# The second Fourier stage's middle channel: a one-row matmul product replaced by a per-token bias in ScalarE's copy

## The chip, the cores and the metric

The kernel runs on one core of one Trainium2 chip. The metric is device time in microseconds, from a program's start to its end, as the median of several runs. A profile is one further execution, with a record of every instruction of every engine. The engines are PE (TensorE, with its weight loads shown as PEld), DVE (VectorE), ACT (ScalarE), POOL (GpSimd) and SP (SyncE, which here only issues DMAs). A DMA can be issued from the queue of several engines; in this kernel nearly all are issued by SyncE, and a few by ScalarE.

## The reference

Eight batches of 576 tokens, eight heads of 64 channels each, all in fp32. An attention of the linear kind comes first, then a Fourier mix with a layer norm and an MLP:

```
q_s = softmax(q, over the head's 64 channels);  k_s = softmax(k, over the 576 tokens)
attn = q_s @ (k_s^T @ v)                       # per batch and head
x  = attn as (8, 576, 512)                     # tokens x channels
u  = x + real(fft(fft(x, over tokens), over channels))
un = (u - mean(u)) / sqrt(var(u) + 1e-6)       # over the 512 channels
out = u + max(un @ w_ch1, 0) @ w_ch2           # 512 -> 2048 -> 512
```

The real part of the two-dimensional transform splits into a cosine product minus a sine product. The first stage, over tokens, makes Z, a cosine part and a sine part of each channel (or sum of channels). The second stage multiplies Z with cosines and sines over channels.

## The kernel before, in words

**Work around the change.** The kernel walks through the eight batches, in two phases. In the first it reads and converts weights, computes the attention of batches 0 and 1 and the MLP of batch 0, and prepares weights for the later batches. In the second a steady rhythm runs: while the MLP of one batch fills TensorE (products of L1544 for the up and down halves, L1641, L1671, with results named `ba`, `bb` and `bc`), the attention, the two Fourier stages and the layer norm of the next batch are worked in between. The MLP products use Strassen-like sums of quarter blocks, so VectorE and GpSimd make operands (L1514, L1555, L1617, L1621, L1678).

**The order is written out by hand.** Each piece of work is a list of steps with planned times (the `steps` and `at(...)` lists in the program's last function, and `timed` for batches 2 to 7). The steps are sorted by planned time and issued under a manual schedule, and every engine then works its own queue strictly in that order. Whatever waits at the head of a queue holds everything behind it. Semaphores order engines against each other. A DMA signals its end on one of eight completion semaphores, which are handed round over all DMAs of the SyncE and ScalarE queues in the order of the script.

**First Fourier stage.** `block` (batch 1, one channel block k at a time) and `blocks` (batches 2 to 7) multiply folded tokens by cosines and sines (`ft`). k = 0 and 1 are the cosine halves of the channels, k = 2 and 3 the sine halves, and k = 4 (`KT`) is the single middle channel, which has a cosine part only and so is one row. In `blocks` the products go to two two-bank PSUM buffers taken from `two()`: one holds the cosines (k = 0, 1, 4), the other the sines (k = 2, 3). The last products are `tails`, L1234, 20 in a batch. ScalarE then copies PSUM to SBUF in `copies(k, part)`:

- part "own" (L1246) makes `Z[b]` for k = 0 to 3, 256 of a batch's own tokens wide, and `Zr` for k = 4, one row of 256;
- part "shared" (L1249, L1250) makes `ZT` for k = 0 to 3 and `ZTr` for k = 4. These are the mirrored tokens that two batches share; batch b writes the half `W*(b%2)` of 64 columns each, so that an odd batch completes the pair.

The order of both parts over k is 2, 3, 0, 1, 4.

**Second Fourier stage.** `second` builds one mix: `mix_own(b, c)` for c = 0, 1 (128 tokens each), and `mix_shared(p)` once for each pair of batches. A mix is, on TensorE, four products of Z with `cd` (the channel cosines and sines; L1264) into one bank, 128 tokens by 512, and a fifth product, L1267, which adds the middle channel. Its left operand is a 128-row tile whose rows but the first stay zero (`Zr`, `ZTr`), and its right one has 129 columns, so that to each token the row's value is added in the cosine half, with a sign that alternates over the frequencies. After the products, `copy` (L1273) has ScalarE move the sine half to SBUF in the tile `sn`. `sums` (L1281) then has VectorE make cosine minus sine and cosine plus sine, and L1282 the two end columns. `adds` adds the result to x. In an odd batch the shared mix comes third, and in batch 7 it comes first.

**Around it.** After the mixes stand the norm (`norm`: statistics L1343 on VectorE, normalisation L1359 on ScalarE for the first batches, transposes L1365 on PE in batch 1) and the MLP of that batch. SyncE's queue around batch 1 holds the loads of the next batch's values (`vt`, L689, eight 32-token pieces in `values_to`), and stores of prepared weight sums (`w1s`, L452 and L455 and `w2s`, L455, in `combine`), with later loads of the same (L476). VectorE works on the weight sums at L449.

Of the kernel before, what the change touches and what calls it, by code (L numbers as in the profile page):

```python
# [46 lines left out]
P = 128  # L47
# [91 lines left out]
class _Block:  # L139
    def __init__(self, ctx, tc, q, kT, v, w1, w2, ft, cd, out):  # L140
        self.nc, self.tc = tc.nc, tc
        self.q, self.kT, self.v, self.w1, self.w2, self.out = q, kT, v, w1, w2, out
        self.ft_dram, self.cd_dram = ft, cd
        nc = self.nc
        pool = lambda name, **kw: ctx.enter_context(tc.tile_pool(name=name, bufs=1, **kw))
        self.const, self.work, self.small = pool("const"), pool("work"), pool("small")
        self.open_banks = []
        self.banks(0)
        ctx.callback(lambda: [p.__exit__(None, None, None) for p in self.open_banks[::-1]])
        self.dram = pool("dram", space=bass.MemoryType.DRAM)  # L150
        c = self.const
        self.ident = c.tile([P, P], F32, name="ident")
        make_identity(nc, self.ident[:])
        self.eps = c.tile([P, 1], F32, name="eps")
        nc.gpsimd.memset(self.eps[:], LN_EPS)
        self.pairs = []
        for b in range(2):
            t = c.tile([P, NR, DH + 1], F32, name=f"pairs{b}")
            (nc.vector if b else nc.gpsimd).memset(t[:], 1.0)
            self.pairs.append(t)  # L160
        self.sn = []
        for i in range(2):
            t = c.tile([P, NN], F32, name=f"sn{i}")
            nc.gpsimd.memset(t[:], 0.0)
            self.sn.append(t)

        self.ZT = c.tile([P, KT, P], F32, name="ZT")

        self.Zr, self.ZTr = c.tile([P, HD], F32, name="Zr"), c.tile([P, P], F32, name="ZTr")
        for t in (self.Zr, self.ZTr):  # L170
            nc.gpsimd.memset(t[:], 0.0)
        self.kb = c.tile([P, NR, 4, NC * Q], F32, name="kb")
        kb = self.kb[:].rearrange("p r g s -> p (r g s)")
        self.kss = [kb[:, i * NC * P:(i + 1) * NC * P].rearrange("p (c n) -> p c n", n=P) for i in range(NR)]
        self.vt = c.tile([P, NC, 2 * P + 3], F32, name="vt")

        self.T, self.F = c.tile([P, 2 * NR, 4, NT], F32, name="T"), c.tile([P, 2 * NR, P + W], F32, name="F")
        nc.gpsimd.memset(self.T[:], 0.0)
        nc.gpsimd.memset(self.F[:], 0.0)

        self.sign = c.tile([P, 1], F32, name="sign")
        nc.gpsimd.memset(self.sign[:], -1.0)
        nc.gpsimd.memset(self.sign[0:W], 1.0)
        d = self.dram
        self.w1s = [d.tile([P, 7, HD], F32, tag=f"w1s{p}", name=f"w1s{p}", bufs=1) for p in range(NP)]
        self.w2s = d.tile([7, P, NP, HD], F32, tag="w2s", name="w2s", bufs=1)

        self.w2d = d.tile([P, len(DEEP), GT], F32, tag="w2d", name="w2d", bufs=1)
        self.plan, self.base = [], {}
        for at in range(1, B + 1):  # L190
            self.base[at] = len(self.plan)
            self.plan += [self.w1s[p][:].rearrange("p a n -> p (a n)") for pair in PAIRS for p in pair]
            one = lambda m: self.w2s[WB_AT[m]].rearrange("p a n -> p (a n)")
            first = self.first_deep(at)
            self.plan += [one(m) for m in (ORDER if at == 1 else (1, 2) if at == B else (1,))]
            if at > 1:
                for i in range(first, len(DEEP), 4):
                    self.plan.append(self.w2d[:, i:min(i + 4, len(DEEP)), :].rearrange("p a n -> p (a n)"))
            if at == B:
                self.plan.append(one(4))  # L200

        self.big = c.tile([P, 3 * NF * D], F32, name="big")
        self.fifth = self.big[:, 3 * NF * D - 5 * P:3 * NF * D - P].rearrange("p (r n) -> p r n", n=P)
        nc.gpsimd.memset(self.fifth[0:64], 0.0)
        part = lambda i: self.big[:, i * NF * D:(i + 1) * NF * D].rearrange("p (f n) -> p f n", n=D)
        self.w1sb, self.w2sb, self.h0 = part(0), part(1), part(2)
        self.ft = c.tile([P, 4 * NM], F32, name="ft")
        self.cd = c.tile([P, 5 * QD + 1], F32, name="cd")
        self.xs, self.live, self.stream = {}, {}, {}
        self.turns = 0  # L210
        self.eo, self.unT, self.Z = {}, {}, {}
        self.unused = None
        self.pairs_used = []

        self.later = []

        self.words = [self.work.tile([P, 2, D], F32, tag=n, name="words", bufs=k) for n, k in (("xs", 2), ("x", 4), ("x", 4))]
# [928 lines left out]
    def block(self, b, k):  # L1146
# [26 lines left out]
        def copies():  # L1173
            pz, Z = box.pop(), self.Z[b]
            z, zt = (self.Zr[0:1], self.ZTr[0:1]) if k == KT else (Z[0:n, k, :], self.ZT[0:n, k, :])
            nc.scalar.copy(paired(z), interleaved(pz[:, NT - 1:NT - 1 + 2 * ME])[:, 0:P, :])

            at = W * (b % 2)
            nc.scalar.mul(paired(zt[:, at:at + Q]), interleaved(pz[:, 0:2 * MO])[:, 0:NT - 1, ::-1],
                          -1.0 if sines else 1.0)  # L1180
            nc.scalar.copy(paired(zt[:, at + Q:at + W]), interleaved(pz[:, 0:2 * ME])[:, NT - 2::-1, ::-1])

        return [(0, times), (1.4, copies)]

    def blocks(self, b):

# [50 lines left out]
        def copies(k, part, copy=nc.scalar.copy):  # L1237
            n, sines, Z = {3: QD - 1, 4: 1}.get(k, P), k in (2, 3), self.Z[b]
            z, zt = (self.Zr[0:1], self.ZTr[0:1]) if k == KT else (Z[0:n, k, :], self.ZT[0:n, k, :])
            flat = box[sines][0:n].rearrange("p a n -> p (a n)")  # L1240
            odd, even = place(k, 1).start, D + place(k, 0).start

            def both(x, y, size, step=1):
                return bass.AP(flat.tensor, flat.offset + x, [flat.ap[0], [step, size], [y - x, 2]])
            if part == "own":
                copy(paired(z), both(odd + NT - 1, even + NT, P))  # L1246
                return
            w = W * (b % 2)
            nc.scalar.mul(paired(zt[:, w:w + Q]), both(even, odd, NT - 1), -1.0 if sines else 1.0)  # L1249
            nc.scalar.copy(paired(zt[:, w + Q:w + W]), both(even + NT - 1, odd + NT - 2, NT - 1, -1))  # L1250

        return own, tails, copies, early, sine

    def second(self, z, zr, adds, two=True, apart=None):

        nc, V = self.nc, self.nc.vector
        cd, box = self.cd, []

        def times():
            banks = apart() if apart else [self.acc((P, D), two)] * 2  # L1260
            parts = (1, 0, QD), (0, QD, QD + 1), (2, NN + QD - 1, QD), (3, NN, QD - 1)
            for k, at, size in (parts[2], (3, HD, QD), *parts[:2]) if apart else parts:
                rows, pm = QD - 1 if k == 3 else P, banks[k > 1]
                nc.tensor.matmul(pm[:, at:at + size], lhsT=z(k)[0:rows], rhs=cd[0:rows, at:at + size], start=True,  # L1264
                                 stop=(k != 0))
                if k == 0:
                    nc.tensor.matmul(pm[:, at:at + size], lhsT=zr(), rhs=cd[:, D:], start=False, stop=True)  # L1267
            box.extend(banks)

        def copy():  # L1270
            sn = self.sn[self.turns % 2]
            self.turns += 1
            nc.scalar.copy(paired(sn[:, 0:HD]), interleaved(box.pop()[:, HD:]))  # L1273
            box.append(sn)

        def sums():
            pm, sn = box
            two = self.halves()
            a = interleaved(pm[:, 0:2 * (QD + 1)])[:, 0:QD, :]
            for i, op in enumerate((ALU.subtract, ALU.add)):  # L1280
                V.tensor_tensor(out=paired(two[:, i * NN + 1:(i + 1) * NN]), in0=a, in1=paired(sn[:, 1:NN]), op=op)  # L1281
# [14 lines left out]

    def mix_shared(self, p):
        return self.second(lambda k: self.ZT[:, k, :], lambda: self.ZTr[:],
                           [lambda lo, hi: self.added(self.xshared(p), hi, lo)])

    def mix_own(self, b, c):
        s = slice(c * P, (c + 1) * P)
# [4 lines left out]
            t = self.two()  # L1307
            return [t[:, 0, :], t[:, 1, :]]

        return self.second(lambda k: self.Z[b][:, k, s], lambda: self.Zr[:, s], adds, apart=None if b else apart)  # L1310

    def norm(self, g):

# [520 lines left out]
def kernel(ctx: ExitStack, tc: tile.TileContext, q, kT, v, w1, w2, ft,  # L1834
# [3 lines left out]
    def timed(t, order, g):  # L1838
# [12 lines left out]
        for k, dt in ((2, 0), (3, 0.9), (0, 4.4), (1, 4.6), (4, 6.4)):  # L1851
            steps.append((t + soon + dt, lambda k=k: own(k)))
        steps.append((t + soon + 6.6, tails))
        for i, k in enumerate((2, 3, 0, 1, 4)):
            for j, part in enumerate(("own", "shared")):
                steps.append((t + soon + 7.8 + 0.2 * i + 1.0 * j, lambda k=k, part=part: copies(k, part)))
        mixes = [blk.mix_own(b, c) for c in range(2)]
# [73 lines left out]
    t = 0  # L1931
# [62 lines left out]
```

## Time and profile before

| | |
|---|---|
| median of three timed runs | 1006.84 us (1006.43 to 1006.99) |
| profiled execution, span from first to last instruction | 1006.6 us |
| PE busy in the profiled execution | 995.6 us, 99% |
| PEld busy | 855.7 us, 85% |
| DVE busy | 718.6 us, 71% |
| ACT busy | 493.2 us, 49% |
| POOL busy | 442.9 us, 44% |
| granted TensorE clock | 1.000 |

The profiled execution has no other time of its own than the span. In the rows that are quoted below, L12 is line 12 of the kernel, `xN` the number of instructions in a group, and `a<-b` the tile written and the tiles read. A row of the timeline begins with the start in us from the start of the span and the duration in us; where instructions of one kind that follow each other are put together (`x4`), the duration is from the first's start to the last's end. In square brackets stand the idle time of that engine just before, and what ended it.

### The profile page before, as it was taken

The page shows a single profiled execution, that of the slowest core. Times are in us where ns is not written, and L with a number is a line of the kernel's source. Part 1 is how long each engine was busy: PE and PEld are TensorE (multiplying, and loading weights), DVE is VectorE, ACT ScalarE, POOL GpSimd, SP SyncE. Part 2 cuts the span into 40 slices and gives each one's busy share as a digit, 9 for nine tenths or more (in the row PEclk, how much of TensorE's full clock was granted, in tenths as well). Part 3 has the DMA queues.
Part 4 walks back from the last instruction along what each step waited for, and adds up shares of the span by engine and source line. Part 5 has one row for each costly group of instructions (what it writes and reads, how often), then busy time and mean ns, then how long its engine had stood idle before and what let it go on. Part 6 is the DMA issues. An engine that isn't in the chain of part 4 may idle for free.

```text
span 1006.6 us, 19808 instructions
## 1 busy us (share of the span) xinstructions
PE 995.6 (99%) x7562; PEld 855.7 (85%) x7562; DVE 718.6 (71%) x1356; ACT 493.2 (49%) x1277; POOL 442.9 (44%) x445
## 2 busy tenths in 40 slices
PE   8999999999999999999999999999999999999998
PEld 6844464888888899889988998899889998998897
DVE  6898898666765887588756877688667945685563
ACT  4585642872468228832775177625772342151200
POOL 4263420357535637664655465655646450040000
PEclk9999999999999999999999999999999999999999
DMA  9987499687989666975677577847753765674573
GB/s 300 258 281 245 158 240 346 205 243 226 342 283 272 230 230 219 266 237 210 251 220 242 206 269 237 253 174 270 231 204 135 267 213 200 224 265 172 183 256 132
DMA packets 123559, 236.37 MB, mean 235 GB/s; under 512 B 24184, under 2 KB 88440, under 8 KB 112840
## 3 DMA queue, kind: packets, MB, share of 16 engines
q1 hardware_dynamic: 123096, 234.58, 71.0%
q8 instruction: 60, 0.98, 0.4%
q14 instruction: 35, 0.29, 0.1%
q10 hardware_dynamic: 288, 0.26, 0.1%
q0 software_dynamic: 80, 0.26, 0.1%
HBM read 199.94 MB, written 39.06 MB: 237 GB/s over the span
## 4 chain that ended last, share of the span: by engine, by line
PE 87%; DVE 7%; ACT 3%; DMA 1%; issue 1%; SPq 0%; POOL 0%; DVEq 0%; POOLq 0%
PE bb L1544 16%; PE ba L1544 11%; PE bc L1544 11%; PE bb L1671 10%; PE ba L1671 7%; PE bc L1671 7%; PE bb L1641 5%; PE bc L1479 2%; PE bb L1760 2%; PE two L840 2%; PE one L755 2%; PE two L1207 1%; PE two L1264 1%; PE ba L1479 1%; PE bc L1760 1%; PE ba L1760 1%
## 5 line engine op out<-in xcount | busy, mean ns | idle before, releaser
L1544 PE MATMUL bb<-unT,big 128*128 128x256 f32 x768 | 183.3, 380 | 0.0
L1544 PEld LDWEIGHTS bb<-unT,big 128*128 128x128 f32 x768 | 144.8, 190 | 20.7 <-DVE u L1514 0.7
L1556 ACT ACTIVATE big<-big 128x512 f32<-128x512 f32 x96 | 59.8, 629 | 147.6 <-DVE big L1555 141.0
L1544 PE MATMUL ba<-unT,big 128*128 128x256 f32 x512 | 123.9, 382 | 0.0
L1544 PE MATMUL bc<-unT,big 128*128 128x256 f32 x512 | 121.5, 380 | 0.1
L817 ACT ACTIVATE qT<-q 32x128 f32<-32x128 f32 x384 | 117.9, 307 | 5.9 <-DVE q L807 0.8
L1544 PEld LDWEIGHTS bc<-unT,big 128*128 128x128 f32 x512 | 96.9, 190 | 13.7 <-DVE big L1555 0.5
L1544 PEld LDWEIGHTS ba<-unT,big 128*128 128x128 f32 x512 | 95.5, 190 | 13.9 <-issue 0.5
L1514 DVE TENSOR_TENSOR u<-bb,s 128x512 f32<-128x512 f32 x66 | 45.2, 685 | 85.0 <-PE bb L1544 66.5
L1671 PE MATMUL bb<-big 128*128 128x128 f32 x848 | 103.8, 276 | 0.2 <-DVE u L1678 0.2
L1671 PEld LDWEIGHTS bb<-big 128*128 128x128 f32 x848 | 98.9, 192 | 1.0 <-DVE u L1678 1.0
L1390 POOL COPY unT<-unT 32x256 f32<-32x256 f32 x98 | 42.0, 428 | 90.2 <-DVE unT L1382 85.9
L1621 POOL TENSOR_TENSOR x<-x,big 128x512 f32<-128x512 f32 x45 | 60.9, 1368 | 46.0 <-DVE big L1678 19.7
L1617 DVE TENSOR_TENSOR big<-big 128x512 f32<-128x512 f32 x98 | 79.9, 842 | 0.0
L1671 PE MATMUL ba<-big 128*128 128x128 f32 x640 | 79.0, 276 | 0.0
L1671 PEld LDWEIGHTS ba<-big 128*128 128x128 f32 x640 | 75.0, 192 | 0.8
L1390 ACT COPY unT<-unT 32x256 f32<-32x256 f32 x126 | 50.7, 402 | 31.3 <-DVE unT L1382 29.5
L804 POOL TENSOR_TENSOR q<-q,qm 128x512 f32<-128x512 f32 x24 | 25.8, 1073 | 88.2 <-DVE qm L799 53.1
L405 POOL TENSOR_TENSOR big<-big 128x512 f32<-128x512 f32 x24 | 30.4, 1268 | 68.4 <-ACT big L1556 68.4
L1641 PE MATMUL bb<-big 128*128 128x256 f32 x256 | 58.3, 379 | 0.0
L1555 DVE TENSOR_TENSOR big<-bc,u 128x512 f32<-128x512 f32 x64 | 44.0, 688 | 17.3 <-PE bc L1544 16.4
L1641 PEld LDWEIGHTS bb<-big 128*128 128x128 f32 x256 | 48.0, 190 | 6.1
(336 smaller groups left out, 1917.9 us busy)
## 6 DMA issues: line engine op xcount, KB each, us to landing
big<-w2d SPq DMA_DIRECT2D x67, 1024.0 KB, 4.6
big<-w1s SPq DMA_DIRECT2D x64, 896.0 KB, 4.7
big<-w2s SPq DMA_DIRECT2D x16, 1024.0 KB, 4.8
big<-in_w_dram SPq DMA_DIRECT2D x21, 512.0 KB, 6.0
w2d<-big SPq DMA_DIRECT2D x42, 256.0 KB, 6.5
kb<-in_kT_dram SPq DMA_DIRECT2D x28, 320.0 KB, 7.8
q<-in_q_dram SPq DMA_DIRECT2D x28, 256.0 KB, 6.0
vt<-in_v_dram SPq DMA_DIRECT2D x84, 80.0 KB, 2.7
```

Source lines behind the costliest of these rows:

```text
L405: e1.tensor_tensor(out=to(4), in0=at(2), in1=at(3), op=ALU.add)
L817: nc.scalar.activation(to[t, i * Q:i * Q + Q], one, ACT.Exp)
L1390: copy(to, of)
L1514: plus = lambda t: V.tensor_tensor(out=temp(t), in0=box["bb"][:], in1=box["s1"][:], op=ALU.add)
L1544: nc.tensor.matmul(bank()[:, i, :], lhsT=w[:, WA_AT[m], k * P:(k + 1) * P], rhs=self.unT[g][:, B_AT[m], k, :], start=first and i == 0 and ...
L1555: steps = [(0, lambda: V.tensor_tensor(out=hp(i), in0=bank()[:], in1=u()[:], op=ALU.add)), (0.8, lambda: nc.scalar.activation(hp(i), hp(i) ...
L1556: (0.8, lambda: nc.scalar.activation(hp(i), hp(i), ACT.Relu))]
L1617: e.tensor_tensor(out=to(o), in0=to(x), in1=to(y), op=op)
L1621: E.tensor_tensor(out=x, in0=x, in1=tile(m), op=ALU.add)
L1641: nc.tensor.matmul(box[name][:, i, :], lhsT=h[p][:, A_AT[m], i * P:(i + 1) * P], rhs=self.stream[n][:, p, :], start=p == 0 and (m != 1 or ...
L1671: nc.tensor.matmul(box[place[n]][:, i, :], lhsT=own(m)(A_AT[n])[:, f, :], rhs=w[:, r // 2, r % 2 * P:r % 2 * P + P], start=first and f == ...
L1760: nc.tensor.matmul(bank()[:, i, :], lhsT=h[p][:, A_AT[m], i * P:(i + 1) * P], rhs=w[:, p, :], start=first and i == 0 and p == 0, stop=p == ...
```

## The change

Batches 1 to 7 drop the fifth product; batch 0's two own mixes keep it (`column=None`). In its place:

- `column(name, row)` turns a row of PSUM results that has been copied to SBUF (`Zr`, `ZTr`) into a column over partitions. It issues one DMA for each 128 tokens, from ScalarE's queue: two for `Zr` (tile `zc`), one for `ZTr` (tile `zt`, in odd batches, when the pair is complete). That is 18 DMAs in all. It returns a step for GpSimd that writes the negated column beside it. The tiles have one buffer each.
- In `blocks` the columns are issued behind the row copies, and the order of the copies over k becomes 4, 2, 3, 0, 1, so that the rows are copied first. GpSimd's negation (`blk.minus`) gets its place 11.5 after the first products. In `block` (batch 1) the columns follow the copies of k = 4, and the negation comes at 3.
- In `second` ScalarE no longer copies the sine half but the cosine half: one plain copy of the even columns, and two `Identity` activations of the odd ones, with the column or its negation as the bias for each partition (token). VectorE's sums then read the sine half directly from PSUM, and the cosine half from `sn`. The end columns come from `sn` too.

```diff
@@ block (batch 1)
+            if k == KT:
+                box.extend([self.column("zc", self.Zr[0:1]), self.column("zt", self.ZTr[0:1])])
+
+        return [(0, times), (1.4, copies)] + [(3, lambda: [f() for f in box])] * (k == KT)
-        return [(0, times), (1.4, copies)]
@@ blocks (batches 2 to 7), copies
                 copy(paired(z), both(odd + NT - 1, even + NT, P))
+                if k == KT and b:
+                    self.minus = [self.column("zc", z)]
                 return
...
+            if k == KT and b % 2:
+                self.minus.append(self.column("zt", zt))
@@
+    def column(self, name, row):
+        nc, n = self.nc, row.shape[1] // P
+        t = self.small.tile([P, 2, n], F32, tag=name, name=name, bufs=1)
+        for i in range(n):
+            nc.scalar.dma_start(t[:, 0, i:i + 1], row[:, i * P:(i + 1) * P])
+        self.columns[name] = t
+        return lambda: nc.gpsimd.tensor_scalar(out=t[:, 1], in0=t[:, 0], scalar1=-1.0, scalar2=None, op0=ALU.mult)
@@ second, times
-                                 stop=(k != 0))
-                if k == 0:
+                                 stop=(k != 0 or not whole))
+                if k == 0 and whole:
                     nc.tensor.matmul(pm[:, at:at + size], lhsT=zr(), rhs=cd[:, D:], start=False, stop=True)
@@ second, copy
-            nc.scalar.copy(paired(sn[:, 0:HD]), interleaved(box.pop()[:, HD:]))
+            if whole:
+                nc.scalar.copy(paired(sn[:, 0:HD]), interleaved(box.pop()[:, HD:]))
+                box.append(sn)
+                return
+            pm, (t, i) = box.pop(), column()
+            nc.scalar.copy(sn[:, 1:NN:2], pm[:, 0:QD])
+            for j in range(2):
+                nc.scalar.activation(sn[:, 2 * j:NN:4], pm[:, QD + j:HD + 1:2], ACT.Identity, bias=t[:, j, i:i + 1])
             box.append(sn)
@@ second, sums
+            if not whole:
+                s = pm[:, HD + QD:]
+                s = bass.AP(s.tensor, s.offset, [s.ap[0], [1, QD], [1 - QD, 2]])
+                for i, op in enumerate((ALU.subtract, ALU.add)):
+                    V.tensor_tensor(out=paired(two[:, i * NN + 1:(i + 1) * NN]), in0=paired(sn[:, 1:NN]), in1=s, op=op)
+                ends = two[:, 0:2 * NN].rearrange("p (i n) -> p i n", i=2)[:, :, ::HD]
+                V.tensor_copy(ends, sn[:, ::HD].unsqueeze(1).to_broadcast([P, 2, 2]))
+                box.append(two)
+                return
@@ timed (batches 2 to 7)
-        for i, k in enumerate((2, 3, 0, 1, 4)):
+        steps.append((t + soon + 11.5, lambda: [f() for f in blk.minus]))
+        for i, k in enumerate((4, 2, 3, 0, 1)):
             for j, part in enumerate(("own", "shared")):
                 steps.append((t + soon + 7.8 + 0.2 * i + 1.0 * j, lambda k=k, part=part: copies(k, part)))
```

More of the change, by code (lines that the diff above doesn't have):

```diff
@@ L209, in __init__ @@
         self.xs, self.live, self.stream = {}, {}, {}
-        self.turns = 0
+        self.turns, self.columns = 0, {}
         self.eo, self.unT, self.Z = {}, {}, {}
@@ L1250, in copies, with second @@
             nc.scalar.copy(paired(zt[:, w + Q:w + W]), both(even + NT - 1, odd + NT - 2, NT - 1, -1))
+            if k == KT and b % 2:
+                self.minus.append(self.column("zt", zt))
         return own, tails, copies, early, sine
-    def second(self, z, zr, adds, two=True, apart=None):
+    def column(self, name, row):
[5 more added lines that the diff above has]
+        return lambda: nc.gpsimd.tensor_scalar(out=t[:, 1], in0=t[:, 0], scalar1=-1.0, scalar2=None, op0=ALU.mult)
+    def second(self, z, zr, adds, two=True, apart=None, column=None):
         nc, V = self.nc, self.nc.vector
         cd, box = self.cd, []
+        whole = column is None
         def times():
@@ L1298, in mix_shared @@
         return self.second(lambda k: self.ZT[:, k, :], lambda: self.ZTr[:],
-                           [lambda lo, hi: self.added(self.xshared(p), hi, lo)])
+                           [lambda lo, hi: self.added(self.xshared(p), hi, lo)], column=lambda: (self.columns["zt"], 0))
     def mix_own(self, b, c):
@@ L1308, in apart @@
             return [t[:, 0, :], t[:, 1, :]]
-        return self.second(lambda k: self.Z[b][:, k, s], lambda: self.Zr[:, s], adds, apart=None if b else apart)
+        return self.second(lambda k: self.Z[b][:, k, s], lambda: self.Zr[:, s], adds, apart=None if b else apart,
+                           column=(lambda: (self.columns["zc"], c)) if b else None)
     def norm(self, g):
```

## The prediction

> **What bounds the kernel now.** I read the page's busy times and its chain first, then a table of busy time by stage, then the timeline around each use of the product that goes.
>
> ```profile
> span 1006.6 us, 19808 instructions
> PE 995.6 (99%) x7562; PEld 855.7 (85%) x7562; DVE 718.6 (71%) x1356; ACT 493.2 (49%) x1277; POOL 442.9 (44%) x445
> PE 87%; DVE 7%; ACT 3%; DMA 1%; issue 1%; SPq 0%; POOL 0%; DVEq 0%; POOLq 0%
> ```
>
> TensorE is busy 99% of the span, and 87% of the chain that ends last is PE. The table by stage (stretch, length, then each engine's busy time) says whether there are gaps in which lost time could be made good.
>
> ```profile
> 150.00:180.00 30.00, 29.89 (x95) 16.10 (x94) 24.34 (x57) 11.64 (x27) 1.71 (x1) 1.00 0.91 314
> 460.00:565.00 105.00, 105.00 (x911) 96.66 (x910) 76.03 (x141) 58.66 (x162) 60.98 (x59) 1.00 0.72 235
> 565.00:780.00 215.00, 215.00 (x1861) 197.99 (x1861) 156.75 (x299) 120.18 (x333) 123.36 (x120) 1.00 0.65 220
> ```
>
> PE has no gap at all from 460 to 780 us. So a product taken off PE is worth its whole time, and a microsecond for which PE is held costs a whole microsecond, because PE takes its work in order. The question is therefore what the 18 products cost, and whether the new copies and transfers hold PE. I add the terms to the profiled span of 1006.6; the three timed runs have their median 0.24 us above it, at 1006.84, and I carry that 0.24 along.
>
> **What is removed.** This is batch 4, from its last first-stage products to the first second-stage mix. Columns: start, duration, engine, line, operation.
>
> ```profile
> 455.85 1.00 PE L1234 MATMUL two<-ft,eo 17*128 17x145 f32 x20
> 456.70 1.20 ACT L1246 COPY Z<-two 128x256 f32<-128x256 f32 x4 [0.57 <-PE two L1234]
> 456.79 1.86 PEld L1671 LDWEIGHTS ba<-big 128*128 128x128 f32 x16
> 457.75 0.36 ACT L1246 COPY Zr<-two 1x256 f32<-1x256 f32 x1
> 457.77 2.94 POOL L1617 TENSOR_TENSOR unT<-big,unT 128x512 f32<-128x512 f32 x2
> 458.02 0.18 ACT L1249 ACTIVATE ZT<-two 128x32 f32<-128x32 f32 x1
> ...
> 458.26 0.16 ACT L1250 COPY ZT<-two 127x32 f32<-127x32 f32 x1
> ...
> 458.57 0.53 PEld L1264 LDWEIGHTS two<-cd,Z 128*128 128x128 f32 x4
> ...
> 459.01 0.30 PEld L1267 LDWEIGHTS two<-cd,Zr 128*128 128x128 f32 x2
> ...
> 459.68 1.87 PEld L1671 LDWEIGHTS bb<-big,unT 128*128 128x128 f32 x16
> ...
> 462.79 0.75 DVE L1281 TENSOR_TENSOR eo<-two,sn 128x256 f32<-128x256 f32 x2
> ```
>
> A mix is five products, two records each. Ten records fill 458.57 to 459.68, 0.111 us each, so one product is 0.222 us. Batches 1 to 7 have 14 own mixes and 4 shared ones: 18 x 0.222 = 4.0 us off PE.
>
> **What holds PE in batches 3 to 7.** A mix writes into the two-bank buffer that held the sine products. It may start when ScalarE has read the last of them, the second ZT copy pair (the 127-row one): 458.26 + 0.16 = 458.42 before, 0.15 us ahead of PE at 458.57. That margin is all there is. The change puts the one-row copy Zr first, behind it two column DMAs issued by ScalarE itself, then the four Z, then ZTr (in odd batches with a third DMA), and only then the ZT pairs. What does an issue cost ScalarE? The trace has two, near the end:
>
> ```profile
> L1821 ACTq EVENT_SEMAPHORE x2: 17/17/17, 963.9 to 992.2; - x2
> L1821 ACTq DMA_DIRECT2D out_dram<-x x2: 360/366/373, 967.7 to 998.3; - x2
> DMA to landing us min/median/max: 1.7/1.7/1.7
> ```
>
> Those move 128 rows; a column has 128 elements, also one piece for each partition, so I take 0.37 us. The bound below is a bare queue event, 0.02. With t counted from 456.70, the start of the Z copies: Zr must await the last four of the 20 records of L1234, about (1.00 - 0.28) / 19 = 0.04 apart (0.28 is the overlap of the last, an estimate), so 0.15. It ends at 0.15 + 0.36 = 0.51; the DMA awaits that, 0.05 for the signal (an estimate); two issues bring 1.30. Four Z at 0.26 (from 456.70 to 457.75) bring 2.35, ZTr 0.15 more, the two ZT pairs 0.40 (from 458.02 to 458.42), a signal 0.05: PE may start at 2.95. Before it started at 458.57, which is 1.87. PE is held for 1.08 us in batches 4 and 6. In 3 and 5 the third issue adds its wait for the ZTr copy (0.10), a signal and 0.37: 1.60. Against 0.44 and 0.67 saved there, the nets are +0.64 and +0.93 each.
>
> Batch 7 mixes the shared tokens first, which need the last ZT pair, and that now stands behind a copy (L1685) of the main work:
>
> ```profile
> 772.98 1.20 ACT L1246 COPY Z<-two 128x256 f32<-128x256 f32 x4 [0.57 <-PE two L1234]
> ...
> 775.06 0.52 PEld L1264 LDWEIGHTS two<-cd,ZT 128*128 128x128 f32 x4
> ...
> 775.16 0.37 ACT L1685 COPY s<-ba 128x256 f32<-128x256 f32 x1 [0.15 <-PE ba L1671]
> ...
> 776.39 1.87 PEld L1671 LDWEIGHTS bb<-big,unT 128*128 128x128 f32 x16
> ```
>
> ZT can start at 3.02; three pairs 0.45, the L1685 copy 0.27, the last pair 0.25, a signal 0.05: 4.04 against 2.08 before, +1.96. This mix shrinks from 1.33 to 8 x 0.111 = 0.89, the two others save 0.44: net +1.08. Batches 3 to 7 together: 2 x 0.93 + 2 x 0.64 + 1.08 = +4.22.
>
> **Batch 2** has room:
>
> ```profile
> 242.66 1.20 ACT L1246 COPY Z<-two 128x256 f32<-128x256 f32 x4 [3.30 <-PE two L1234]
> ...
> 246.09 0.63 PEld L1264 LDWEIGHTS two<-cd,Z 128*128 128x128 f32 x4
> ```
>
> 242.66 + 2.95 = 245.61, 0.48 before PE gets there. It saves 0.44.
>
> **Batch 1: the transfers' semaphores.** Eight completion semaphores are handed round over all of SyncE's and ScalarE's DMAs in the order of the script, and an issue waits for the DMA that had its semaphore before. In the listing of the built program the script places the three columns among the eight vt loads of batch 2's values:
>
> ```
> SP   L689  DMA vt<-in_v      (7th of 8)   waits DMAHW4 = 208, which the first zc column raises
> SP   L689  DMA vt<-in_v      (8th)        waits DMAHW5 = 208, the second zc column
> SP   L453  DMA w1s<-big                   waits DMAHW7 = 208, the zt column
> ```
>
> SyncE ran well ahead of that place:
>
> ```profile
> 133.22 0.31 SPq L689 DMA_DIRECT2D vt<-in_v_dram  x1
> 134.94 0.31 SPq L689 DMA_DIRECT2D vt<-in_v_dram  x1
> 135.30 0.42 SPq L452 DMA_DIRECT2D w1s<-big  x1
> ...
> 138.90 0.40 SPq L455 DMA_DIRECT2D w1s<-big  x1
> DMA to landing us min/median/max: 4.5/4.5/4.5
> ...
> 139.00 0.16 ACT L1181 COPY ZTr<-acc 1x32 f32<-1x32 f32 x1
> ...
> 143.37 0.32 SPq L476 DMA_DIRECT2D big<-w1s  x1
> 144.74 0.50 SPq L455 DMA_DIRECT2D w2s<-spare  x1
> ...
> 152.00 0.76 DVE L449 TENSOR_TENSOR spare<-big 128x256 f32<-128x256 f32 x2 [1.87 <-DMA w2s<-spare]
> ...
> 159.40 2.23 ACT L1359 ACTIVATE eo<-x,mv,std 128x512 f32<-128x512 f32 x3 [0.44 <-DVE mv L1343]
> ...
> 160.26 0.14 PEld L1365 LDWEIGHTS tr<-ident,eo 128*128 128x128 f32 x1 [0.25 <-ACT eo L1359]
> ```
>
> (The 4.5 is the landing of the store at 138.90.) The seventh vt load went at 133.22. Now it waits for a column issued when ScalarE is past 139.16 and landed 1.7 us later: 140.9. Behind it in SyncE's queue stand the eighth load, six w1s stores, a w1s load that awaits their landing, and the w2s stores. From the seventh load, 0.3 for each vt and 0.5 for each store, the last store goes at about 143.9 instead of 138.90, and lands at 148.4; everything from 143.37 on is 5.0 us late. VectorE already waited 1.87 us for the w2s store; it now waits to about 157. Behind that wait in VectorE stand the statistics of batch 1, then ScalarE's normalisation (159.40), whose first 0.81 us releases PE's transpose at 160.26 with nothing to spare. PE stands still, and the 0.67 saved in this batch goes into the same wait: net +5.0. Below, if the last store lands in 1.7 like the ScalarE store, the term is +2.2. Above, if a column takes as long as the slowest small load,
>
> ```profile
> q<-in_q_dram SPq DMA_DIRECT2D x12, 64.0 KB, 7.1
> ```
>
> it is 5.0 + 5.4 = +10.4. I take 5.0, since the DMA engines are nearly idle while SyncE is held.
>
> [...]
>
> **What else is added** costs nothing while it is covered. Three ScalarE instructions for one in a copy, under 0.6 us more: in batch 4 the sums at 462.79 wait for PE's next product. GpSimd's negation stands behind its work until 457.77 + 2.94 = 460.71, and the columns have landed by then (456.70 + 0.56 + 0.74 + 1.7 = 459.70); the second bias copy awaits it, and nothing urgent stands behind either. If a column took 7.1 us, that cover would be gone, and VectorE's sums would be about 1 us late in each batch. The sums and the end copy on VectorE keep their sizes.
>
> **Sum.** -0.44 (batch 2) + 4.22 (3 to 7) + 5.0 (batch 1) = +8.8: 1006.6 + 0.24 + 8.8 = 1015.6 us.
>
> **Rivals.**
> *Issues cost ScalarE almost nothing* (0.02). The held time shrinks to 0.38, 0.55 and, in batch 7, a net of 0.03; batches 3 to 7 become -0.33, the sum +4.2: 1011.1. Against it stand the 360 to 373 ns rows, which are of a queue that had nothing behind them. [...]
> *Batch 1 takes no harm*: VectorE's wait at 152.00 does not lengthen. Then -0.67 - 0.44 + 4.22 = +3.1: 1009.9. It would need the stores to catch up 5 us; the idle DMA engines speak for some of it, the queue order against.
> *Columns land late* (7.1 us): 8.8 + 5.4, 1021, with some more from the sums.
> *Not slower: the held time is given back.* If PE, once late, found later waits shorter, only the 4.0 saved would stay: 1002.8. It decides from the point where PE has about 9 us of waits after 160 us for things that do not move with it. The stages without a gap speak against it; what PE idles after 780 lies mostly in the tail.
>
> **Chances.** Forecast 0.54, cheap issues 0.12, no harm in batch 1 0.12, late columns 0.13, given back 0.09. The range 1009.0 to 1020.5 takes in the forecast with the bound +2.2, both smaller cases and part of the late columns. About 0.2% (2 us) is what a measurement of this kernel can tell from no change. Faster 0.09, the last rival; the same 0.05, out of the low side of the third case; slower 0.86.
>
> **What would show it.** 36 fewer PE records, and 18 column DMAs of about 0.37 us in ScalarE's queue. PE's first mix product in batches 3 to 7 about 1.1 and 1.6 us after the ba products, released by a ZT copy. The seventh vt load near 141, the transposes of L1365's successor near 165. I am wrong if SyncE passes the vt loads by 136, if PE shows no wait ahead of the first mixes, or if the first transpose still comes near 160.

## The result, and the profile after

| | before | changed |
|---|---|---|
| median | 1006.75 us (1006.43 to 1006.99) | 1022.67 us (1020.91 to 1025.22) |
| ratio, with 95% interval | | 1.016 [1.0145, 1.0175] |
| profiled execution, span | 1006.6 us | 1019.1 us |
| mean granted TensorE clock, each run | 1.000 (profiled) | 0.998, 0.995, 0.997, 0.997 |

The kernel became 15.9 us slower. The forecast was 8.8 slower, and 1022.67 lies above its range. The page of the changed kernel (lines L1671, L1267 and L1365 of before are L1705, L1284 and L1399 here):

```profile
span 1019.1 us, 19818 instructions
PE 994.9 (98%) x7526; PEld 852.5 (84%) x7526; DVE 720.3 (71%) x1356; ACT 503.2 (49%) x1313; POOL 446.0 (44%) x456
PE 73%; DVE 14%; ACT 4%; DMA 3%; issue 2%; POOL 1%; ACTq 1%; SPq 1%; DVEq 0%; POOLq 0%
```

36 PE records are gone, as intended, and TensorE's share of the chain that ends last fell from 87% to 73%: other engines now end waits that TensorE did not have. The waits by engine name two of them (total us, times, longest):

```profile
PEld two L1281 <- ACT ZT L1254: 10.7, 6, 2.8
PEld tr L1399 <- ACT eo L1393: 4.7, 2, 4.2
```

The first is the hold at the first mix of a batch, 10.7 us in six batches; the second is batch 1. Both are counted as the forecast's rows are, between weight loads (PEld); the matmuls, which end later, stand still for a shorter time. The same stretches by stage, with granted clock as the third number from the end:

```profile
150.00:180.00 30.00, 25.68 (x72) 12.80 (x71) 22.80 (x52) 7.83 (x16) 1.72 (x1) 0.94 0.97 338
460.00:565.00 105.00, 103.69 (x898) 95.19 (x897) 74.84 (x142) 59.60 (x165) 60.09 (x60) 1.00 0.72 235
565.00:780.00 215.00, 211.56 (x1823) 194.03 (x1823) 157.38 (x298) 122.83 (x342) 124.14 (x123) 1.00 0.64 219
```

TensorE has gaps where it had none, and between 150 and 180 us its clock was cut. Batch 4 in the timeline:

```profile
462.29 1.00 PE L1236 MATMUL two<-ft,eo 17*128 17x145 f32 x20
463.35 0.36 ACT L1248 COPY Zr<-two 1x256 f32<-1x256 f32 x1 [0.78 <-PE two L1236]
463.74 1.13 ACTq L1265 DMA_DIRECT2D zc<-Zr  x2
464.91 1.20 ACT L1248 COPY Z<-two 128x256 f32<-128x256 f32 x4 [1.20 <-issue]
...
466.37 0.16 ACT L1254 COPY ZT<-two 127x32 f32<-127x32 f32 x1
...
466.58 0.97 PEld L1281 LDWEIGHTS two<-cd,Z 128*128 128x128 f32 x8 [1.50 <-ACT ZT L1254]
```

This is the forecast's sequence, step for step, with two issues of 1.13 us together where 0.74 was put. TensorE starts no weight load for 1.50 us (the matmuls stand still for 1.31 of them). Batch 1:

```profile
129.89 10.22 SPq L689 DMA_DIRECT2D vt<-in_v_dram  x6
...
147.51 0.48 SPq L455 DMA_DIRECT2D w2s<-spare  x1
...
154.61 0.76 DVE L449 TENSOR_TENSOR spare<-big 128x256 f32<-128x256 f32 x2 [5.40 <-DMA w2s<-spare]
...
162.87 0.65 PEld L1399 LDWEIGHTS tr<-ident,eo 128*128 128x128 f32 x4 [4.23 <-ACT eo L1393]
```

SyncE, which had left its vt loads by 135, is held in them until 140. VectorE waits 5.40 us for the w2s store instead of 1.87, and TensorE starts no weight load for 4.23 us ahead of the transposes (no matmul runs for 3.40). The semaphores in the trace fit the forecast. The DMAs of SyncE and ScalarE signal on eight of them in turn (numbers 101 and 104 to 110), and the seventh vt load waits for 107, which the first column's transfer raises: it was issued at 139.18, when that semaphore was full at 139.17, and the eighth at 139.81, when the second column's (108) was full at 139.79. What follows that gap was in no step of the forecast:

```profile
158.00:163.00 5.00, 1.60 (x5) 0.51 (x4) 4.46 (x14) 1.29 (x3) 0.00 (x0) 1.00 0.74 261
163.00:167.00 4.00, 4.00 (x12) 2.54 (x13) 3.86 (x11) 3.98 (x7) 0.00 (x0) 0.57 0.99 326
```

A mean of 0.57 over 4.00 us is 3.4 us at half clock (from 163.00 to 166.41 us the granted clock is 0.50): 1.7 us lost.

**Where the time lies.** Comparing the start of each weight load in the two traces, with the removed products left out, gives how late the changed kernel is at each place:

| stretch | forecast | trace |
|---|---|---|
| up to 111 us, where nothing was changed | 0 | -1.9 |
| batch 1, 111 to 170 us | +5.0 | +5.5, of which 1.7 half clock |
| batch 2, to 249 us | -0.4 | +0.1 |
| batches 3 to 7, to 790 us | +4.2 | +9.0 |
| the rest | 0 | -0.2 |
| sum | +8.8 | +12.5 |

The -1.9 is no effect of the change: the profiled execution of before had a slow opening, and the other profiled kernels that are compared with it in this way are 0.6 to 1.9 us ahead of it at 111 us as well. In later runs, which list time and span of each, the time is 1.8 us longer than the span, so that execution took some 1008.4 us (the spans of other runs of before lie between 1003.4 and 1008.0, most of them from 1004 to 1006). From 12.5 to the measured 15.9 the rest is this 1.6, and 1.8 because by its clock (0.997 against 0.998) the median run has about one more stretch at half clock than the profiled one, an estimate.

### The profile page after: what moved, and what is told of

It reads as the page before. It is cut to its first block, busy times and chain, and to the rows that moved or that the text cites. A ratio compares the mean times of both kernels' runs of the same rounds, so it can differ in the third digit from the quotient of the medians.

```text
span 1019.1 us, 19818 instructions
## 1 busy us (share of the span) xinstructions
PE 994.9 (98%) x7526; PEld 852.5 (84%) x7526; DVE 720.3 (71%) x1356; ACT 503.2 (49%) x1313; POOL 446.0 (44%) x456
## 4 chain that ended last, share of the span: by engine, by line
PE 73%; DVE 14%; ACT 4%; DMA 3%; issue 2%; POOL 1%; ACTq 1%; SPq 1%; DVEq 0%; POOLq 0%
PE bb L1578 15%; PE ba L1578 10%; PE bc L1578 10%; PE bb L1705 8%; PE bb L1675 5%; PE bc L1705 5%; PE ba L1705 4%; DVE big L1651 2%; PE bc L1513 2%; PE two L840 2%; ACT qT L817 2%; PE two L1209 1%; PE one L755 1%; PE ba L1794 1%; DMA big<-in_w_dram 1%
## 5 line engine op out<-in xcount | busy, mean ns | idle before, releaser
L1705 PE MATMUL bb<-big 128*128 128x128 f32 x848 | 104.2, 276 | 0.9 <-DVE u L1712 0.6
L1705 PEld LDWEIGHTS bb<-big 128*128 128x128 f32 x848 | 98.9, 192 | 2.4 <-DVE u L1712 2.4
L1705 PE MATMUL ba<-big 128*128 128x128 f32 x640 | 79.0, 276 | 0.0
L1705 PEld LDWEIGHTS ba<-big 128*128 128x128 f32 x640 | 75.0, 192 | 0.8
```

Of the source, the lines that this page charges most:

```text
L1705: nc.tensor.matmul(box[place[n]][:, i, :], lhsT=own(m)(A_AT[n])[:, f, :], rhs=w[:, r // 2, r % 2 * P:r % 2 * P + P], start=first and f == ...
```

## Experiments

All ratios are to the kernel before, run on the same chip in the same round.

| kernel | median us | ratio [95%] |
|---|---|---|
| batch 1 with the product | 1019.97 | 1.013 [1.0099, 1.016] |
| rows copied last | 1013.24 | 1.0064 [1.0047, 1.0081] |
| columns from SyncE | 1007.53 | 1.001 [1.0, 1.0019] |
| no columns | 1007.72 | 1.0009 [0.9999, 1.0018] |
| batch 1's columns from GpSimd | 1018.42 | 1.0121 [1.0104, 1.0139] |
| rows last, SyncE | 1006.41 | 0.9995 [0.9986, 1.0005] |
| gaps filled | 1016.27 | 1.009 [1.0073, 1.0106] |
| rows last, no columns | 1005.83 | 0.9989 [0.9979, 0.9998] |
| rows last, SyncE, two adds on GpSimd | 1005.33 | 0.998 [0.997, 0.9989] |
| rows last, SyncE, batch 1 with the product | 1006.46 | 0.9989 [0.9981, 0.9998] |
| both of these | 1005.88 | 0.9989 [0.998, 0.9998] |
| half columns | 1034.51, one run | |

**1. Batch 1 keeps the product.**

```diff
-            if k == KT:
-                box.extend([self.column("zc", self.Zr[0:1]), self.column("zt", self.ZTr[0:1])])
...
-                           column=(lambda: (self.columns["zc"], c)) if b else None)
+                           column=(lambda: (self.columns["zc"], c)) if b > 1 else None)
```

> Batch 1 keeps the fifth product and has no columns; batches 2 to 7 as in the changed kernel. Theory: two separate losses. In batches 3 to 7 TensorE is held at its first mix (9.0 us net between 250 and 797 us in the changed kernel's trace); in batch 1 SyncE is held behind the columns, the transposes come late, and the gap on TensorE is followed by a stretch at half the granted clock. This kernel keeps the first and loses the second: 1006.8 + 9.0 = about 1015.8 us, clock 1.000, runs within 0.5 us of each other, and the first transpose back near 160 us. Rival: the half clock and the scatter have nothing to do with batch 1: clock still below 0.999 and 1018 or more.

The batch-1 part came out (the transposes are on time), the clock part did not. The four runs took 1016.44, 1018.11, 1021.84 and 1022.22 us at clocks of 1.000, 0.998, 0.996 and 0.995. The run without half clock is 0.6 us above the expected 1015.8; the others take 1.7, 5.4 and 5.8 us longer than it, where the granted clock alone accounts for about 2, 4 and 5. So batch 1's long gap is not the only one that a cut of the clock follows. In the profiled run the cut came with the hold at the first mix of batch 3 (the timeline, then two windows, with the clock at 1.00 and 0.72):

```profile
353.19 1.26 PEld L1279 LDWEIGHTS two<-cd,Z 128*128 128x128 f32 x8 [2.35 <-ACT ZT L1252]
348.00:352.00 4.00, 3.02 (x37) 2.65 (x36) 2.54 (x3) 1.99 (x8) 3.60 (x3) 1.00 0.81 262
352.00:356.00 4.00, 2.81 (x15) 2.81 (x16) 0.00 (x0) 2.04 (x12) 1.33 (x3) 0.72 0.04 2
```

**2. Rows copied last in batches 2 to 7**, with the DMAs behind the ZT copies.

```diff
-        for i, k in enumerate((4, 2, 3, 0, 1)):
+        for i, k in enumerate((2, 3, 0, 1, 4)):
...
-                if k == KT and b:
-                    self.minus = [self.column("zc", z)]
...
-            if k == KT and b % 2:
-                self.minus.append(self.column("zt", zt))
+            if k == KT and b:
+                self.minus = [self.column("zc", self.Zr[0:1])]
+                if b % 2:
+                    self.minus.append(self.column("zt", zt))
```

> Batches 2 to 7: copies in the order of the kernel before (2, 3, 0, 1, 4), and the column DMAs issued only behind the last ZT copies; batch 1 as in the changed kernel. Theory: the hold at the first mix is the time that ScalarE spends on the row copy and the DMA issues ahead of the ZT copies, so it goes, and the 15 products of these batches are saved: 1006.8 - 3.3 + 6.9 (what batch 1 costs in the changed kernel) = about 1010.4 us; the first mix of batches 3 to 7 is no later against the products before it than in the kernel before. Rival: the columns now land late for the bias copies, and the wait moves there: the hold appears at the second or third mix, and 1013 to 1018.

The hold is gone: no wait of TensorE for ZT is left in the list. So what stood ahead of the ZT copies, the row copy and the issues, is its cause; experiment 3 tells the two apart. But the median is 2.8 us above the expected, and the waits show a part of it:

```profile
PEld tr L1399 <- ACT eo L1393: 4.5, 2, 4.2
PEld bb L1705 <- DVE u L1712: 4.0, 10, 0.7
```

Batch 1's gap of 4.2 stays, as meant, and three of four runs have clocks of 0.997 and 0.998. TensorE's waits for VectorE's evictions at L1712 add up to 4.0 us, against 2.4 in the changed kernel and 1.0 before; the issues now stand ahead of ScalarE's later copies and the columns land later, and which of the two causes them was not separated.

**3. All columns from SyncE's queue.**

```diff
-            nc.scalar.dma_start(t[:, 0, i:i + 1], row[:, i * P:(i + 1) * P])
+            nc.sync.dma_start(t[:, 0, i:i + 1], row[:, i * P:(i + 1) * P])
```

> All columns issued from SyncE's queue instead of ScalarE's, all else as in the changed kernel. Theory: ScalarE loses 1.1 to 1.7 us of issuing a batch and only the row copy ahead of the others stays, so TensorE is held 0.4 us instead of 1.5 to 2.8: batches 3 to 7 cost about -1 instead of +9; batch 1 is no better, since SyncE itself now waits for the row: about 1012 to 1014 us. Rival one: the hold comes from the new order of the copies, not from the issues: still near 1022. Rival two: SyncE, waiting for the rows, brings the MLP's weight loads late: waits of TensorE's products for loads, 1015 or more.

Better than either theory or rivals: 15 us come back by naming another queue. An issue takes as long there (0.57 us in the median), but delays no copy (SyncE's queue in batch 1, one line's durations, TensorE's wait):

```profile
125.18 9.60 SPq L689 DMA_DIRECT2D vt<-in_v_dram  x8
...
138.77 1.26 SPq L1265 DMA_DIRECT2D zc<-Zr  x2
...
L1265 SPq DMA_DIRECT2D zc<-Zr x14: 544/572/659, 138.8 to 773.9; - x14
PEld two L1281 <- ACT ZT L1254: 1.6, 5, 0.8
```

The hold falls from 10.7 to 1.6 us, what the row copy alone costs (experiment 4, with no issue at all, has the same 1.6). In batch 1 the expectation was wrong: SyncE passes its eight vt loads freely, from 125.18 to 134.78, because in its own queue the columns come behind them, at 138.77. What an issue takes of the queue's engine is 0.57 us here, and with TensorE waiting for that engine the issues were most of the hold, 9.1 of 10.7 us. The rest of the 15 us is batch 1 and the half clock.

**4. No columns.** The bias is a constant, so the result lacks the middle channel in batches 1 to 7.

```diff
-        for i in range(n):
-            nc.scalar.dma_start(t[:, 0, i:i + 1], row[:, i * P:(i + 1) * P])
+        nc.gpsimd.memset(t[:, 0], 0.0)
```

> The column DMAs are left out, and the bias is a constant zero, so the middle channel is left out of the result in batches 1 to 7; all else as in the changed kernel (order of the copies, three copies for one, VectorE's sums from PSUM, the negation). Theory: with no issue and no semaphore shared with SyncE, only the row copy ahead of the others costs anything: 1006.8 - 4.0 + 5 x 0.4 = about 1004.8 us, clock 1.000. Rival: the new order and the longer copies are what hold TensorE: 1012 or more.

No hold but 1.6 us, clock 0.999 or more, and still no gain: 1007.72, not 1004.8. The DMAs explain the loss, but without them the products' 4.0 us do not arrive either. This became the second question, taken up in 6 to 8.

**5. Batch 1's columns from GpSimd's queue.**

```diff
-                box.extend([self.column("zc", self.Zr[0:1]), self.column("zt", self.ZTr[0:1])])
+                box.extend([self.column("zc", self.Zr[0:1], nc.gpsimd), self.column("zt", self.ZTr[0:1], nc.gpsimd)])
```

> Batch 1's three columns are issued from GpSimd's queue, whose DMAs have completion semaphores of their own; all else as in the changed kernel. Theory: what batch 1 loses comes from the eight shared semaphores alone, so SyncE passes the vt loads by 136 us as in the kernel before, VectorE's wait for the w2s store stays under 2.5 us, and the kernel costs what the one with the product kept in batch 1 costs: 1016 us and 1.7 more for each stretch at half the granted clock. Rival: the late transposes come from ScalarE's or VectorE's own order (columns, negation, three copies for one): the gap of 4.2 us ahead of the transposes stays, and 1020 or more.

```profile
124.10 9.56 SPq L689 DMA_DIRECT2D vt<-in_v_dram  x8
158.83 0.42 PEld L1399 LDWEIGHTS tr<-ident,eo 128*128 128x128 f32 x4 [1.17 <-ACT eo L1393]
```

SyncE is through its loads at 133.7, the transposes come at 158.83 after 1.17 us instead of 4.23. The copies, the negation and the columns are the same; the semaphores are others (in the changed kernel's trace GpSimd's DMA signals on 111, none of the eight), and ScalarE is free of the three issues. That second difference cannot be what lets SyncE through, since in the changed kernel the first of them began at 137.16, after SyncE is through here. So the shared semaphores are shown to be batch 1's cause. The four runs took 1017.85 to 1020.29 us, at clocks of 0.996 to 0.998.

**6. Rows last and SyncE together.**

> Columns from SyncE's queue, and in batches 2 to 7 the row copies last again (order 2, 3, 0, 1, 4) with the DMAs behind the ZT copies. Theory: neither hold is left; of the 4.0 us of products a part is given back where TensorE then waits for VectorE's sums (L1712), as the kernel with no columns shows (its trace falls back from 2.4 us early at 250 to 1.6 us early at 800): 1005.5 to 1006.5, the best of these kernels and about the kernel before. Rival: columns that start after the ZT copies land too late for the bias copies, the sums are late, and TensorE waits: 1009 or more.

1006.41 us: both holds are gone, and the kernel is where before was, no better. **With no columns at all** in the same order:

> No column DMAs, the bias a constant zero (the middle channel is left out of the result in batches 1 to 7), and in batches 2 to 7 the row copies last again. This is the change with nothing to pay for the columns. Theory A: a product taken off TensorE is worth its whole time: 1006.9 - 4.0 = 1002.9. Theory B: half or more is given back, since TensorE then waits for VectorE at L1712 and for ScalarE elsewhere: 1005 to 1006.5. Rival: the three copies for one and VectorE's sums with their other operand order cost more than the products: 1007 or more, as with the row copies first.

1005.83: of 4.0 us about 1.1 arrive (0.2 to 2.1 by the interval). Theory B holds. TensorE's waits in this kernel, and below them the same waits before:

```profile
PEld bb L1704 <- DVE u L1711: 2.3, 8, 0.4
PEld bb L1577 <- DVE u L1547: 1.6, 4, 0.8
PEld tr L1398 <- ACT unT L1407: 1.3, 1, 1.3
PEld tr L1398 <- ACT eo L1392: 1.1, 2, 0.8
```

```profile
PEld bb L1671 <- DVE u L1678: 1.0, 4, 0.4
PEld bb L1544 <- DVE u L1514: 0.7, 3, 0.3
PEld tr L1365 <- ACT unT L1374: 0.9, 1, 0.9
PEld tr L1365 <- ACT eo L1359: 0.3, 1, 0.3
```

6.3 against 2.9 us: these waits are 3.4 us longer, about as much as does not arrive. In a trace they follow the saving: TensorE comes earlier to a place that VectorE (or, in batch 1, VectorE's wait for the w2s store) sets. By the starts of the weight loads, what batches 1 to 5 save is all lost again by 600 us; what arrives is most of what batches 6 and 7 save.

**7. Two adds of the shared mixes on GpSimd.** If VectorE gives the saving back, less work for it must let the saving through.

```diff
-                           [lambda lo, hi: self.added(self.xshared(p), hi, lo)], ...
+                           [lambda lo, hi: self.added(self.xshared(p), hi, lo, self.nc.gpsimd if p else None)], ...
```

> As the kernel with the columns on SyncE's queue and the rows copied last, and the two adds of each shared mix of batches 3, 5 and 7 go from VectorE to GpSimd. Theory: what the products save is given back where TensorE waits for VectorE's evictions (L1712, 2.4 us in 8 places, against 1.0 at the same line in the kernel before), and VectorE has no gap in the stretch ahead of it; 0.67 us less work for it there lets more of the saving through: the waits at L1712 sum to under 1.5 us, and the time is 1005.5 to 1006.0. Rival: VectorE is not what gives it back, or GpSimd's slower adds hold what follows on GpSimd or the norm: 1006.4 or more.

```profile
PEld bb L1705 <- DVE u L1712: 1.8, 5, 0.6
```

1005.33, ratio 0.998 [0.997, 0.9989]: faster than expected, with the waits at 1.8 us somewhat above. Its interval overlaps that of experiment 6 a little (0.9986 to 0.9989), so the step from the one to the other is likely, not certain; that this version beats the kernel before, by 0.2%, is shown.

**8. Batch 1 with the product**, on top of experiments 6 and 7.

> Columns on SyncE's queue and the rows copied last, and batch 1 keeps the product. Theory: in batch 1 the 0.67 us saved is lost again ahead of the transposes (the trace with the columns there goes from 1.3 us early at 148 to 0.3 early at 160), so keeping the product there costs nothing or gains up to 0.3: 1006.0 to 1006.4. Rival: the saving of batch 1 does last to the end: 1007.1.

> The two before together: columns on SyncE's queue, rows last, batch 1 with the product, the adds of the shared mixes of batches 3, 5 and 7 on GpSimd. If both theories hold: 1005.2 to 1005.8, about 0.1% under the kernel before; otherwise 1006.4 or more.

1006.46 and 1005.88, both 0.9989: the first is a little above its band and the second just above, and neither is told from its partner with the columns. What batch 1's products are worth stays open within about 1 us.

**9. The gaps filled.** To experiment 1 come 38 products of constants on TensorE, ahead of the first mixes.

```diff
+            if fill:
+                t = self.acc((P, D))
+                for _ in range(fill):
+                    nc.tensor.matmul(t[:, 0:P], lhsT=cd[:, 0:P], rhs=cd[:, 0:P], start=True, stop=True)
             banks = apart() if apart else [self.acc((P, D), two)] * 2
```

> Batch 1 keeps the product, as in the first experiment, and ahead of the first mix of batches 3 to 7 TensorE does 6 to 10 extra products of constants (0.22 us each, 38 in all, results unused) in the time in which it otherwise stands still. Theory: the stretches at half clock come from gaps of over 1.5 us on TensorE; with the gaps filled none is left: granted clock 0.999 to 1.000 in every run, all runs within 1.5 us of each other near 1016.5, although 8.4 us of work were added. Rival: the half clock does not come from gaps: runs scatter over 1016 to 1022 as without the extra products; or the extra products cost their own time: 1024.

1016.27 us against 1019.97: 8.4 us of extra work on TensorE, and the median is 3.7 us lower (the two intervals, 1.0073 to 1.0106 and 1.0099 to 1.016, just overlap). The clock is 0.999 to 1.000 in the four runs, and no stage's window shows less than 1.00. They scatter over 2.6 us instead of 5.8 (1.5 was expected). With the gaps filled the half clock is gone, so here it comes from TensorE's gaps. The 1.5 us of the theory was the author's estimate; the shortest gap that a fall was seen to follow is experiment 1's, of 2.35 us.

**10. Half columns.** Twice as many issues of half the size, on experiment 1.

```diff
-        for i in range(n):
-            nc.scalar.dma_start(t[:, 0, i:i + 1], row[:, i * P:(i + 1) * P])
+        for i in range(2 * n):
+            nc.scalar.dma_start(t[P // 2 * (i % 2):P // 2 * (i % 2 + 1), 0, i // 2:i // 2 + 1],
+                                row[:, i * P // 2:(i + 1) * P // 2])
```

> Batch 1 with the product; batches 2 to 7 as in the changed kernel, but each column moved by two DMAs of 64 numbers instead of one of 128 (four or six issues a batch on ScalarE instead of two or three). Theory: an issue costs ScalarE its 0.48 to 0.58 us whatever its number of pieces: issues of about 0.5, TensorE's gap ahead of the first mix 2.6 us in even and about 3.8 in odd batches instead of 1.5 and 2.2. Rival: the cost goes by pieces: issues of about 0.28, the gaps unchanged.

One line's durations (min, median, max in ns), batch 4's issues, TensorE's wait, and the clock:

```profile
L1263 ACTq DMA_DIRECT2D zc<-Zr x24: 470/608/1052, 242.8 to 795.3; - x24
464.94 2.71 ACTq L1263 DMA_DIRECT2D zc<-Zr  x4
PEld two L1279 <- ACT ZT L1252: 20.5, 6, 4.2
core 0: 1032.7 us, clock 0.992
```

An issue of 64 numbers takes 0.47 us at the least and 0.61 in the median, one of 128 took 0.48 and 0.58 in the changed kernel, so the cost goes by issue. Two more of them lengthen the hold in batch 4 from 1.50 to 3.08 us, more than the 2.6 expected, and with holds of up to 4.2 us in six batches, 20.5 us together, the clock falls to 0.992.

## Why the prediction was wrong

The direction and both mechanisms were right; the size was not. Three steps failed: the price of an issue (0.37 us put, 0.48 to 0.58 measured), the premise that on a TensorE without a gap a product taken off is worth its whole time and a microsecond of hold costs one (other waits took back some of the saving), and the half clock, which was missing altogether. Of the 7.1 us between the forecast and the result, batches 3 to 7 hold +4.8, batch 2 +0.5, the half clock in the median run about +3.4, and batch 1 -1.2; the remaining -0.4 lies outside these stretches.

- **What holds PE in batches 3 to 7**: right in every step but the issue's size. Forecast 0.37 us, from two stores at the kernel's end; measured (min, median, max in ns):

```profile
L1265 ACTq DMA_DIRECT2D zc<-Zr x14: 477/576/1066, 137.2 to 785.0; - x14
L1265 ACTq DMA_DIRECT2D zt<-ZTr x4: 477/478/557, 138.4 to 787.0; - x4
```

Batch 4 shows the arithmetic: against t = 2.95 TensorE could start at 3.44, and 0.39 of that 0.49 are the two issues. The 0.05 put for a signal had no row behind it; the trace has 0.03 from the Zr copy to the issue (463.71 to 463.74) and 0.05 from the 127-row ZT copy to TensorE (466.53 to 466.58). The holds were 1.50 for 1.08 (batches 4 and 6), about 2.2 for 1.60 (3 and 5) and 2.83 for 1.96 (7): 10.2 us instead of 7.3.
- **Batch 2 has room**: it had 0.48 us, and was held 0.49, because its two issues took 1.58 us where 0.74 was put:

```profile
246.86 1.58 ACTq L1265 DMA_DIRECT2D zc<-Zr  x2
250.16 0.97 PEld L1281 LDWEIGHTS two<-cd,Z 128*128 128x128 f32 x8 [0.49 <-ACT ZT L1254]
```

The second of them took 1.07 us. It is no wait for its semaphore: the trace has it issued at 247.38, and the transfer that had that semaphore before landed at 240.72. Why it took so long stays open.
- **A product taken off PE is worth its whole time**: this failed. "No gap" in a window of TensorE was read as "bound by TensorE alone". VectorE was busy 14.79 of 15.00 us around the third mix of batch 3, and TensorE just not waiting for it:

```profile
360.00:375.00 15.00, 15.00 (x136) 15.00 (x136) 14.79 (x35) 4.18 (x7) 4.08 (x3) 1.00 0.75 271
```

Experiment 6 put a number on it: about 1.1 of 4.0 us arrive. In batches 3 to 7 the trace has 10.2 of hold and 13 products (2.9) saved, yet +9.0, so 1.7 us were lost in other waits there.
- **Batch 1**: right, with a net of 3.8 us without the half clock, against 5.0. Of the rivals, the one without harm is refuted: by SyncE at 140 and by experiment 5. The changed trace runs 1.9 us ahead when batch 1 begins, and this has to be added to a difference of its times with before. So the w2s store, at 147.51 and 144.74, went 4.7 us later, and the first transpose, at 162.87 and 160.26, came 4.5 us later, close to the 5.0 put. The rest of the difference is that about 0.7 us was made up behind the first transposes.
- **The half clock**: in no step and no rival. The forecast priced a microsecond of hold at a microsecond. The profiled run lost 1.7 us in 3.41 us at 0.50; by the granted clocks of 0.998 to 0.995 the estimate is 1.7 to about 5 us in the four runs, some 3.4 in the median one. By that arithmetic the kernel without it would take about 1019.3 us, inside the range, though with errors of both signs in it.
- **The span**: 0.24 us was carried as the difference of the profiled span and the median. That compared a span with a time, and the profiled run was 1.6 us slower than the median. It did the sum no harm, since the two together are the median of the timed runs, 1006.84.
- **Cheap issues** are refuted by 477 ns as the shortest issue, where that rival put 20 ns; so are **late columns**: by the trace's semaphores the 18 columns landed 1.9 to 5.0 us after their issue began, not 7.1. **Given back** did happen, but to the saving, not to the loss.

## What to carry to other kernels

An engine that copies out of PSUM should not issue DMAs ahead of copies for which TensorE waits: an issue cost 0.5 to 0.6 us of that engine's time, for 64 numbers as for 128, and moving the issues to SyncE's queue took back 15 of the 16 us. Before counting a saving on a saturated engine, look for the second engine that is as full in the same stretch; here VectorE was, and about a fourth of the saving arrived; with work moved off VectorE it was likely more. A gap on TensorE can cost more than its length: the one of 4.23 us here was followed by 3.41 us at a clock of 0.50, 1.7 us more, while three others of 2.19 to 2.83 us in the same trace were followed by none.

## What the runs showed of the hardware

**Half clock after gaps.** Two falls of the granted clock can be placed, and both came with a hold of TensorE. In batch 1 of the changed kernel weight loads paused for 4.23 us (matmuls for 3.40), and the clock was 0.50 for 3.41 us, from 163.00 to 166.41. In experiment 1 they paused for 2.35 us (2.16) ahead of the first mix of batch 3, up to 353.19, and the clock was 0.72 in the mean from 352 to 356 us and 0.93 from 356 to 365. Not every such hold was followed by a fall: in the changed kernel's trace those of 2.19, 2.23 and 2.83 us (2.00, 2.04 and 2.64 between matmuls; batches 3, 5 and 7) were not, nor were those of 1.50 (batches 4 and 6). So length alone does not decide, since 2.83 was followed by none and 2.35 by one. What tells the one kind from the other was not shown.

**Semaphores tie queues together.** In the changed kernel columns on ScalarE's queue held the last two of SyncE's vt loads, although the two move unrelated data: the loads went at 139.18 and 139.81, when the semaphores that they wait for had been filled by the columns at 139.17 and 139.79. SyncE was through at 140.1; with the columns on GpSimd's queue it was through at 133.7 (experiment 5).
